# A new order for the lead and block 0 of a fused attention and two-MLP kernel, with six more groups of dummy matmuls

## The chip, the cores and the metric

The kernel runs on one core of a Trainium2 chip. The metric is device time in microseconds (us) of one execution, and of several executions the median. TensorE (PE) multiplies, VectorE (DVE), ScalarE (ACT) and GpSimd (POOL) work elementwise, and SyncE (SP) issues nearly all DMAs. Each engine runs its own instructions strictly in the order in which the program lists them, and semaphores hold an instruction until its operands are there.

## What is computed

Three layers follow one another, all in fp32:

```python
# r, k, v: (4, 8, 768, 48); w, u: (8, 48)
for t in range(S):                              # decayed linear attention
    cur = einsum('bhd,bhe->bhde', u * kt, vt)
    y[:, :, t] = einsum('bhd,bhde->bhe', rt, state + cur)
    state = w * state + einsum('bhd,bhe->bhde', kt, vt)
x = y.transpose(0, 2, 1, 3).reshape(3072, 384)
h = x @ w_in;  g = relu(h)**2;    x = g @ w_out   # 384 -> 2048 -> 384
h = x @ w_in2; g = h - tanh(h);   x = g @ w_out2  # 384 -> 2048 -> 384
```

To keep fp32 accuracy, both operands of each large product are split into a high and a low part, and three of the four cross products are formed.

## The kernel before

**Blocks.** The 3072 tokens are cut in 24 chunks of 128 and 6 blocks of 512 (four chunks each). A block of an MLP layer walks over 16 slices of the hidden dimension. For slice f, gemm1 (`h.f`, line 687) makes 9 matmuls of 512 columns, ACT and DVE apply the activation and split its result, and gemm2 (line 736 in the first layer, 860 in the second) makes another 9: six on the high part (`g2.f`), three on the low part (`g2l.f`). The attention of the next block's chunks is slipped between the slices of the first layer.

**The lead.** Chunks 0 to 3 start from an empty state and have a path of their own ahead of the first gemm1, the lead. For chunk i: `rk.i` loads r and k (line 196), `v.i` the values (214); DVE makes the product r*k (`pr.i`, 539) and scales k and r by the decay (`k.i`, 545 and 548; `r.i`, 554 and 557); PE forms the bonus sums (`pb.i`, 567), transposes k (`tp.i`, 574), makes the scores of the two head halves (`lb.2i` and `lb.2i+1`, 602), the state (`lc.i`, 650) and the output (`ly.i`, 636). Between them ACT copies out of PSUM (`lbt.i` 578, `kn.i` 584, `lst.i` 668), POOL writes a diagonal (`dg.i`, 351) and DVE masks the scores over it (`lm`, 613). ACT then writes the high part of the chunk's output into the MLP's input (`lx.i`, 659), DVE the low part (`lxl.i`, 663). `tk` (DVE, 281) and `tt` (PE, 291) build a decay table.

**Weights of the first layer.** Slice f is loaded as raw 64-bit numbers (`w.f`, line 75, five buffers) and turned into two fp32 words by ACT and DVE: `c0.f` (ACT, 89), `c1a.f` (DVE, 96), `c1b.f` (DVE, 100), `c2.f` (ACT, 115), `c3.f` (DVE, 121). `h.f` needs `c2.f` at its first matmul and `c3.f` at its seventh. In block 0 this goes on beside the matmuls; in later blocks the weights stay.

**Attention of chunks 4 to 8** lies in block 0: loads `L.i`, scaling `ar`, `ak`, `nk` (DVE 373, 391, 330), scores `b.i` (PE 432), states `sv.i` (PE 447), output `y.i` (PE 513).

**Order.** The program is written without a scheduler's freedom: `first_order`, a string of some 700 items, is walked once and each item issues its instructions, so it fixes every engine's order through the lead and block 0. After it a plain loop takes over. Items `gt` are tiny POOL copies that wait for the DVE result made last before them. Items `fl` are dummy matmuls into an unused half of a PSUM bank:

```python
def fill(n):
    for q in range(n):
        nc.tensor.matmul(side()[:, 256:512], lhsT=zero, rhs=low[0:GP].bitcast(BF16), start=True, stop=True)
"fl": lambda i: fill(4)
```

A first `fill(WARM)` stands ahead of the list, and each `fl` adds four.

Of the kernel before, what the change touches and what calls it, by code (L numbers as in the profile page):

```python
# [1161 lines left out]
```

## Time and profile before

| | |
|---|---|
| three executions | 864.67, 867.27, 870.47 us (median 867.27) |
| the profiled execution | 866.38 us, of which the trace's span is 864.6 us |
| busy share of the span | PE 99%, weight loads 81%, ACT 74%, DVE 71%, POOL 25% |
| mean granted TensorE clock of the profiled execution | 0.996 |
| first gemm1 matmul | 29.98 us after the span's start |

PE's busy share counts a pipelined matmul from its start to its end, so a busy PE may still run slower than it could; its granted clock is a column of its own. The chain that ended last is PE in 97% of the span.

### The profile page before, as it was taken

Reading aid. Unit: us, or ns where it says so; the run is one execution under the profiler, and the core shown is the slowest. Engines: PE = TensorE matmul, PEld = TensorE weight load, DVE = VectorE, ACT = ScalarE, POOL = GpSimd, SP = SyncE. Lnnn points to the kernel's source line nnn. Section 1 sums busy time; section 2 is a strip of 40 time slices with the busy share of each in tenths; the row PEclk is TensorE's granted clock in tenths of the full one; section 3 lists DMA queues with packets and bytes.
Section 4 is the critical chain, followed back from the end, with each engine's and each line's share of the span. In section 5 each row is a group of like instructions: output and inputs, shape, how many; then the busy total and the mean of one; then the engine's idle time right before and its main releaser. Section 6 shows DMA issues by size and latency. Waiting matters only on the chain.

```text
span 864.6 us, 16203 instructions
## 1 busy us (share of the span) xinstructions
PE 856.0 (99%) x6415; PEld 703.1 (81%) x6415; DVE 616.2 (71%) x1101; ACT 639.6 (74%) x1172; POOL 216.5 (25%) x235
## 2 busy tenths in 40 slices
PE   8999999999999999999999999999999999999998
PEld 6788888888888888888888788888888888888886
DVE  6999842504332340515786999999999999999997
ACT  3889575545555555556887988988988988988996
POOL 4342555545554653531010010010010010010000
PEclk8999999999999999999999999999999999999999
DMA  9874331303212220603640100200200200200100
GB/s 315 279 241 154 119 128 55 108 37 104 59 55 91 71 93 37 237 2 110 206 160 13 61 0 1 74 1 0 74 1 1 73 1 1 74 0 1 38 1 36
DMA packets 26539, 67.20 MB, mean 78 GB/s; under 512 B 3424, under 2 KB 12000, under 8 KB 26464
## 3 DMA queue, kind: packets, MB, share of 16 engines
q1 hardware_dynamic: 26176, 65.79, 22.6%
q8 instruction: 50, 0.82, 0.4%
q10 hardware_dynamic: 288, 0.39, 0.1%
q14 instruction: 25, 0.20, 0.1%
HBM read 55.94 MB, written 9.44 MB: 76 GB/s over the span
## 4 chain that ended last, share of the span: by engine, by line
PE 97%; DMA 1%; ACT 1%; DVE 1%; issue 0%; SPq 0%; DVEq 0%; ACTq 0%
PE h L687 45%; PE acc L736 23%; PE o L860 22%; PE y L513 2%; PE sp L432 1%; PE sp L447 1%; DMA first<-in_rk_dram 1%; PE sc L602 1%; PE y L636 1%; PE pt L650 0%; PE pk L567 0%; PE pk L574 0%; ACT x2s L757 0%; DVE hy L799 0%; ACT y L797 0%
## 5 line engine op out<-in xcount | busy, mean ns | idle before, releaser
L687 PE MATMUL h<-xs,w 128*128 128x512 f32 x864 | 211.3, 389 | 0.0
L687 PE MATMUL h<-xt,w 128*128 128x512 f32 x864 | 210.4, 389 | 0.1
L687 PEld LDWEIGHTS h<-xs,w 128*128 128x128 f32 x864 | 162.2, 188 | 34.0
L687 PEld LDWEIGHTS h<-xt,w 128*128 128x128 f32 x864 | 162.0, 188 | 34.0 <-ACT xt L659 0.3
L702 ACT ACTIVATE g<-h 128x512 f32<-128x512 f32 x96 | 57.3, 598 | 130.4 <-PE h L687 99.7
L736 PE MATMUL acc<-ghi,w 128*128 128x512 f32 x576 | 150.2, 394 | 0.0
L860 PE MATMUL o<-ghi,w 128*128 128x512 f32 x574 | 148.1, 390 | 0.0
L860 PEld LDWEIGHTS o<-ghi,w 128*128 128x128 f32 x574 | 107.3, 188 | 23.3 <-ACT ob L884 1.3
L736 PEld LDWEIGHTS acc<-ghi,w 128*128 128x128 f32 x576 | 106.5, 188 | 22.9 <-ACT ghi L710 0.4
L713 POOL TENSOR_TENSOR glo<-g,ghi 128x512 fp32r<-128x512 f32 x64 | 82.6, 1291 | 140.9 <-PE acc L736 78.2
L530 DVE TENSOR_TENSOR xt<-y,xt 128x384 fp32r<-128x384 f32 x20 | 11.1, 557 | 146.9 <-ACT xt L524 146.9
L778 POOL TENSOR_TENSOR xs<-x2f,xs 128x512 fp32r<-128x512 f32 x18 | 24.4, 1357 | 358.3 <-DVE xs L777 358.3
L800 ACT ACTIVATE th<-h 128x512 f32<-128x512 f32 x96 | 57.6, 600 | 41.0 <-DVE hy L799 41.0
L860 PE MATMUL o<-glo,w 128*128 128x512 f32 x287 | 83.3, 392 | 0.3 <-DVE glo L830 0.3
L736 PE MATMUL acc<-glo,w 128*128 128x512 f32 x288 | 82.2, 389 | 0.0
L813 DVE SCALAR_TENSOR_TENSOR hy<-q,hy 128x512 f32<-128x512 f32 x96 | 76.7, 799 | 0.1
L799 DVE SCALAR_TENSOR_TENSOR hy<-h,y 128x512 f32<-128x512 f32 x96 | 65.9, 687 | 14.1 <-ACT y L797 14.0
L818 DVE COPY_PREDICATED hy<-mask,th 128x512 f32<-128x512 uint8 x96 | 70.8, 738 | 0.1
L803 DVE TENSOR_TENSOR th<-h,th 128x512 f32<-128x512 f32 x96 | 66.2, 690 | 6.1 <-ACT th L800 0.7
L801 ACT ACTIVATE q<-y,ba 128x512 f32<-128x512 f32 x96 | 68.6, 714 | 0.0
L804 ACT ACTIVATE q<-y,bb 128x512 f32<-128x512 f32 x96 | 68.5, 713 | 0.0
L807 ACT ACTIVATE mask<-y,bm 128x512 uint8<-128x512 f32 x96 | 68.3, 711 | 0.0
(114 smaller groups left out, 1114.5 us busy)
## 6 DMA issues: line engine op xcount, KB each, us to landing
raw<-in_w_dram SPq DMA_DIRECT2D x32, 768.0 KB, 5.1
rkt<-in_rk_dram SPq DMA_DIRECT2D x20, 512.0 KB, 3.8
x2d<-x2s SPq DMA_DIRECT2D x18, 256.0 KB, 2.3
x2f<-x2d SPq DMA_DIRECT2D x18, 256.0 KB, 3.4
vs<-in_nat_dram SPq DMA_DIRECT2D x40, 112.0 KB, 4.1
out_dram<-ob SPq DMA_DIRECT2D x17, 256.0 KB, 2.4
rnt<-in_nat_dram SPq DMA_DIRECT2D x20, 192.0 KB, 4.2
kn<-in_nat_dram SPq DMA_DIRECT2D x20, 192.0 KB, 4.4
```

The source lines that it names most:

```text
L687: nc.tensor.matmul(h, lhsT=w_in(layer, f, part, kk), rhs=x[:, xpart, kk, :], start=(n == 0), stop=(n == 3 * KK - 1),)
L713: nc.gpsimd.tensor_tensor(lo, g, hi.bitcast(F32), op=ALU.subtract)
L736: nc.tensor.matmul(acc[j][m], lhsT=w_out(1, f, part, m * 128, (m + 1) * 128), rhs=g, start=(f == 0 and n == 0), stop=(f == NF - 1 and n == 2),
L799: nc.vector.scalar_tensor_tensor(out=hy, in0=h, scalar=PK, in1=y, op0=ALU.mult, op1=ALU.mult)
L800: nc.scalar.activation(out=th, in_=h, func=AF.Tanh)
L801: nc.scalar.activation(out=q1, in_=y, func=AF.Square, bias=p2["ba"], scale=1.0)
L803: nc.vector.tensor_tensor(th, h, th, op=ALU.subtract)
L804: nc.scalar.activation(out=q2, in_=y, func=AF.Square, bias=p2["bb"], scale=1.0)
L807: nc.scalar.activation(out=mask, in_=y, func=AF.Sign, bias=p2["bm"], scale=1.0)
L813: nc.vector.scalar_tensor_tensor(out=hy, in0=q2, scalar=PD, in1=hy, op0=ALU.add, op1=ALU.mult)
L818: nc.vector.copy_predicated(hy, mask, th)
L860: nc.tensor.matmul(acc[j][m], lhsT=w, rhs=g, start=(f == 0 and n == 0), stop=n == 2 and f == (NF - 2 if m == KK - 1 and j == NB - 1 else N ...
```

## The change

Two things differ. The number of dummy matmuls at the very start, `WARM`, goes from 28 to 27, and `first_order` is another string. The new one has the same items and six `fl` more (`fl.4` to `fl.9`): 24 more dummy matmuls in the list, 23 more in all. All else is in another order. Its first and last lines, and those of the old one:

```diff
-    WARM = 28
+    WARM = 27
...
-        pr.0 k.0 fl.2 fl.0 r.0 pb.0 tp.0 rk.1 rk.2 pr.2 k.2 v.1 v.0 fl.1 tk.0 gt.5 kn.0 tt.0 pr.1 v.2 tn.0 r.1 k.1
-        ub.0 lbt.0 lb.0 lb.1 pb.1 lbt.1 w.0 c1a.0 dg.0 lm.0 tp.1 lc.0 rk.3 lm.1 lb.2 dg.1 lm.2 kn.1 lst.0 ly.0 r.2
...
-        sq.17 hi.17 s1d.8 s1p.8 d.8 nk.9 m.8
+        tk.0 pr.0 fl.2 fl.0 pb.0 k.0 fl.4 fl.5 fl.6 tp.0 kn.0 r.0 w.0 rk.1 pr.1 r.1 ub.0 fl.1 rk.2 pr.2 lbt.0 v.1 v.0
+        v.2 tt.0 tn.0 dg.0 lb.0 c0.0 pb.1 lbt.1 lb.1 dg.1 k.1 r.2 v.3 lm.0 lm.1 gt.19 tp.1 kn.1 lb.2 lm.2 c1a.0 rk.3
...
+        nr.9 ak.9 h.17 ev.0 rl.17 ar.9 ev.2 sq.17 ns.9 d.9 gt.18 hi.17 gt.4 m.8 nk.9 gt.1
```

What that moves is seen on the engines. First PE, behind the warm-up and ahead of the first scores; before, from the bonus sums of chunk 0 on:

```order
L567 MATMUL pk<-wu,first 64x2 x8
L574 MATMUL pk<-ident,first 128x112 x4
L301 LDWEIGHTS zero
L301 MATMUL pt<-low,zero 128x256
...
L291 MATMUL pt<-ident,kh 64x48 x8
L602 MATMUL sc<-first 64x128 x16
```

and in the changed kernel, from the same place:

```order
L567 MATMUL pk<-wu,first 64x2 x8
L301 LDWEIGHTS zero
L301 MATMUL pt<-low,zero 128x256
...
L574 MATMUL pk<-ident,first 128x112 x4
...
L291 MATMUL pt<-ident,kh 64x48 x8
L602 MATMUL sc<-first 64x128 x8
L567 MATMUL pk<-wu,first 64x2 x8
L602 MATMUL sc<-first 64x128 x8
```

The dots are more dummies of the same two rows: before, four between the transposes (574) and the table (291); now twelve between the sums and the transposes, then four. Eight more stand ahead of `lc.0` and four behind `pb.3`. On DVE, `tk.0` (281) was the eighth instruction of the lead's chunk work, behind the first two chunks to arrive, and is now the first.

Second, SP's queue at the start; before:

```order
L245 DMA wu<-in_w_dram 112x16
L199 DMA first<-in_rk_dram 128x512
L196 DMA first<-in_rk_dram 128x1024 x2
L214 DMA first_v<-in_nat_dram 128x448 x3
L951 DMA ub<-in_u_dram 64x192 x2
L75 DMA raw<-in_w_dram 128x1536
L196 DMA first<-in_rk_dram 128x1024
```

and now:

```order
L245 DMA wu<-in_w_dram 112x16
L199 DMA first<-in_rk_dram 128x512
L75 DMA raw<-in_w_dram 128x1536
L196 DMA first<-in_rk_dram 128x1024
L951 DMA ub<-in_u_dram 64x192 x2
L196 DMA first<-in_rk_dram 128x1024
L214 DMA first_v<-in_nat_dram 128x448 x3
```

The raw weights of slice 0 (768 KB) go ahead of chunk 1's r and k (512 KB), and chunk 2's come behind both.

Third, DVE in block 0 between the weights of slices 2 and 3 (the rows are from `c3.2` to `c3.3`, both line 121); before:

```order
L121 TENSOR_TENSOR w_2_600<-raw,w_2_600 128x768
L96 TENSOR_SCALAR raw<-raw 128x768
L100 SCALAR_TENSOR_TENSOR raw<-raw 128x768 x2
L373 TENSOR_TENSOR rkt<-rkt,tr 112x512
L727 TENSOR_TENSOR glo<-g,ghi 128x512
L121 TENSOR_TENSOR w_3_623<-raw,w_3_623 128x768
```

and now:

```order
L121 TENSOR_TENSOR w_2_622<-raw,w_2_622 128x768
L727 TENSOR_TENSOR glo<-g,ghi 128x512
L96 TENSOR_SCALAR raw<-raw 128x768 x2
L100 SCALAR_TENSOR_TENSOR raw<-raw 128x768
L330 TENSOR_TENSOR kn_98<-kn_98,kt_tab 128x384
L100 SCALAR_TENSOR_TENSOR raw<-raw 128x768
L727 TENSOR_TENSOR glo<-g,ghi 128x512
L96 TENSOR_SCALAR raw<-raw 128x768
L121 TENSOR_TENSOR w_3_673<-raw,w_3_673 128x768
```

Two shifts, one low part and the scaling of keys (330) more stand ahead of `c3.3` there; `ar.4` (373) now stands ahead of `c3.2`.

## Rows read from the trace of the kernel before

**Rows 1.** The page: busy time of each engine, and the chain that ended last

```profile
PE 856.0 (99%) x6415; PEld 703.1 (81%) x6415; DVE 616.2 (71%) x1101; ACT 639.6 (74%) x1172; POOL 216.5 (25%) x235
...
PE 97%; DMA 1%; ACT 1%; DVE 1%; issue 0%; SPq 0%; DVEq 0%; ACTq 0%
```

**Rows 2.** Stretches: us, busy of PE, weight loads, DVE, ACT, POOL; clock; DMA share; GB/s

```profile
0.00:30.00 30.00, 25.36 (x461) 20.05 (x461) 21.61 (x49) 13.82 (x38) 16.17 (x42) 0.89 0.92 314
...
10.00:11.00 1.00, 0.28 (x10) 0.28 (x10) 1.00 (x3) 0.00 (x0) 0.31 (x1) 1.00 1.09 405
11.00:12.00 1.00, 1.00 (x41) 1.00 (x40) 0.96 (x3) 0.40 (x2) 0.09 (x1) 0.85 0.98 373
17.00:18.00 1.00, 1.00 (x24) 0.94 (x24) 0.87 (x3) 0.00 (x0) 0.00 (x0) 0.50 0.98 377
18.00:19.00 1.00, 1.00 (x32) 0.70 (x24) 1.00 (x2) 0.00 (x0) 0.00 (x0) 0.73 0.98 395
30.00:60.00 30.00, 30.00 (x190) 24.56 (x191) 29.29 (x49) 27.36 (x44) 8.70 (x13) 1.00 0.72 236
30.00:150.00 120.00, 119.98 (x1316) 98.24 (x1320) 89.08 (x184) 88.08 (x171) 54.47 (x61) 1.00 0.47 154
```

**Rows 3.** Timeline of PE, lead: start, us, engine, line, tiles, count [idle before <-releaser]

```profile
1.56 5.69 PE L301 MATMUL pt<-low,zero 112*128 112x256 bf16 x36 [1.56 <-POOL low L308]
7.18 0.63 PE L567 MATMUL pk<-wu,first 112*64 112x2 f32 x16
7.75 0.60 PE L574 MATMUL pk<-ident,first 112*128 112x112 f32 x4
8.19 0.60 PE L301 MATMUL pt<-low,zero 112*128 112x256 bf16 x4
10.72 0.49 PE L291 MATMUL pt<-ident,kh 48*64 48x48 f32 x10 [1.93 <-DVE kh L281]
...
19.20 0.67 PE L602 MATMUL sc<-first 48*64 48x128 f32 x16
19.80 0.63 PE L567 MATMUL pk<-wu,first 112*64 112x2 f32 x16
...
22.20 0.63 PE L567 MATMUL pk<-wu,first 112*64 112x2 f32 x16 [0.63 <-ACT first_kn L584]
22.69 0.54 PE L650 MATMUL pt<-first_v,first_kn 128*48 128x48 f32 x16
23.16 1.08 PE L636 MATMUL y<-am,first_v 128*32 128x128 f32 x32
24.17 0.67 PE L602 MATMUL sc<-first 48*64 48x128 f32 x16
...
29.31 0.61 PE L301 MATMUL pt<-low,zero 112*128 112x256 bf16 x4
29.98 2.35 PE L687 MATMUL h<-xt,w 128*128 128x512 f32 x9
```

**Rows 4.** Timeline of DVE, lead

```profile
8.84 0.69 DVE L539 TENSOR_TENSOR first<-first 112x512 f32<-112x512 f32 x1 [1.47 <-DMA first<-in_rk_dram]
...
13.05 1.04 DVE L96 TENSOR_SCALAR raw<-raw 128x768 uint32<-128x768 uint32 x1 [0.46 <-DMA raw<-in_w_dram]
...
26.49 1.45 DVE L613 COPY_PREDICATED am<-low,sc 128x256 f32<-128x256 uint32 x4 [0.33 <-PE sc L602]
```

**Rows 5.** Timeline of DVE, first slices of block 0

```profile
33.82 0.96 DVE L121 TENSOR_TENSOR w<-raw,w 128x768 fp32r<-128x768 f32 x1 [0.43 <-ACT w L115]
...
38.35 0.96 DVE L121 TENSOR_TENSOR w<-raw,w 128x768 fp32r<-128x768 f32 x1
...
44.30 1.03 DVE L96 TENSOR_SCALAR raw<-raw 128x768 uint32<-128x768 uint32 x2
```

**Rows 6.** Timeline of ACT, the same slices

```profile
33.67 0.64 ACT L705 ACTIVATE g<-g 128x512 f32<-128x512 f32 x1
```

**Rows 7.** Timeline of PE, the same slices

```profile
39.74 4.25 PE L687 MATMUL h<-xt,w 128*128 128x512 f32 x18
```

More of the change, by code (lines that the diff above doesn't have):

```diff
@@ L945, in decay_attention_moe_moe_kernel @@
-        sq.17 hi.17 s1d.8 s1p.8 d.8 nk.9 m.8
+        tk.0 pr.0 fl.2 fl.0 pb.0 k.0 fl.4 fl.5 fl.6 tp.0 kn.0 r.0 w.0 rk.1 pr.1 r.1 ub.0 fl.1 rk.2 pr.2 lbt.0 v.1 v.0
+        v.2 tt.0 tn.0 dg.0 lb.0 c0.0 pb.1 lbt.1 lb.1 dg.1 k.1 r.2 v.3 lm.0 lm.1 gt.19 tp.1 kn.1 lb.2 lm.2 c1a.0 rk.3
+        pr.3 fl.7 fl.8 lc.0 w.2 ly.0 lx.0 pb.2 lb.3 w.1 k.2 lb.4 lbt.2 tp.2 lst.0 lc.1 c1b.0 c2.0 lm.3 ly.1 L.4 kn.2
+        pb.3 dg.2 lm.4 r.3 lst.1 fl.9 lb.5 lbt.3 dg.3 c0.1 w.4 k.3 tp.3 c0.2 lb.6 lxl.0 lc.2 c3.0 w.3 lm.5 kn.3 lm.6
@@ new lines, in decay_attention_moe_moe_kernel @@
+        lx.1 lst.2 ly.2 lx.2 lxl.1 w.5 lb.7 lm.7 c1a.1 lc.3 lst.3 nu.4 lxl.2 ly.3 lx.3 nr.4 c1b.1 c2.1 fl.3 lxl.3
+        c1a.2 L.5 c0.4 h.0 c1b.2 rl.0 c3.1 h.1 c2.2 ar.4 sq.0 w.7 c3.2 rd.4 w.6 hi.0 lo.0 rl.1 c1a.3 c1a.4 c0.3 c1b.3
+        sq.1 hi.1 nk.4 gt.13 c1b.4 h.2 rl.2 lo.1 c1a.5 g2.0 c2.3 c3.3 ak.4 w.8 c1a.7 g2.1 g2l.0 c0.5 c2.4 c3.4 h.3
+        sq.2 c0.7 gt.17 h.4 rl.3 hi.2 c1b.5 sq.3 hi.3 gt.9 c2.5 gt.14 c0.8 lo.2 c0.6 g2.2 c1b.7 rl.4 sq.4 c2.7 gt.11
+        ns.4 d.4 c1a.8 c3.5 c1a.6 c1b.6 hi.4 b.4 sv.4 g2.3 h.5 lo.3 rl.5 c2.6 w.9 c3.7 c0.9 g2l.2 g2.4 sq.5 c1b.8 nu.5
@@ new lines, in decay_attention_moe_moe_kernel @@
+        s0p.4 c3.6 L.6 ar.6 h.7 h.6 c1a.9 gt.0 w.10 c1a.10 lo.4 ar.5 hi.5 lo.5 g2l.1 g2l.3 c2.8 g2.5 c3.8 gt.8 s0p.6
+        c1b.9 ak.5 nu.6 s1a.4 rl.6 rl.7 sq.6 s0p.5 h.8 w.12 w.11 nr.5 hi.6 m.4 g2l.4 sq.7 g2.6 lo.6 c2.9 nr.6 c3.9
+        gt.10 c1a.11 hi.7 c0.10 rl.8 c1b.10 h.9 sq.8 w.13 c2.10 s1d.4 w.14 lo.7 c3.10 c0.11 gt.15 g2.7 hi.8 g2l.5
+        g2l.6 c1a.12 lo.8 rd.5 s1p.4 c0.12 c1b.11 nk.5 rl.9 sq.9 c2.11 h.10 rl.10 ns.5 sv.5 s1a.5 c1a.14 y.4 w.15
+        sq.10 nk.6 c3.11 rd.6 b.5 c1b.12 ns.6 hi.10 hi.9 lo.10 d.5 L.7 c1a.13 g2.8 g2l.7 c2.12 h.11 s1p.5 c3.12 gt.5
@@ new lines, in decay_attention_moe_moe_kernel @@
+        ar.7 h.12 g2.10 g2.9 g2l.8 gt.6 c0.15 nu.7 d.6 lo.9 xh.4 xl.4 m.5 rl.11 sq.11 s1d.5 hi.11 sv.6 rl.12 ak.6 y.5
+        rd.7 s1a.6 c0.13 c1b.13 b.6 L.8 c1a.15 sq.12 s0p.7 c0.14 g2.11 hi.12 g2.12 g2l.10 lo.11 c1b.14 c2.13 c3.13
+        lo.12 c1b.15 c2.14 ak.7 s1p.6 xh.5 nr.7 c3.14 c2.15 h.13 nu.8 rl.13 h.14 nk.7 g2l.9 c3.15 g2l.11 s1d.6 m.6
+        xl.5 rl.14 sq.14 hi.14 sq.13 h.15 hi.13 gt.3 ns.7 d.7 sv.7 s1a.7 gt.12 lo.13 rl.15 sq.15 y.6 hi.15 lo.14 b.7
+        g2.13 gt.2 m.7 nr.8 s1d.7 xh.6 g2.14 nk.8 g2l.12 s1p.7 gt.16 g2l.13 g2l.14 lo.15 g2a.15 xl.6 ak.8 ar.8 s0p.8
@@ L946, in decay_attention_moe_moe_kernel @@
+        y.7 L.9 sv.8 ns.8 b.8 d.8 g2b.15 g2c.15 xh.7 xl.7 h.16 s1a.8 s1d.8 s1p.8 ev.1 gt.7 nu.9 rl.16 sq.16 L.10 hi.16
+        nr.9 ak.9 h.17 ev.0 rl.17 ar.9 ev.2 sq.17 ns.9 d.9 gt.18 hi.17 gt.4 m.8 nk.9 gt.1
     """
```

18 lines of the change are left out of this document (removed).

## The prediction

> **What bounds the kernel now.** I read the page first. PE is busy for 99% of the span and is 97% of the chain that ended last [rows 1], so only what shortens PE's own sequence can help. Then the busy time by stretches. From 30 to 150 us PE is busy for 119.98 of 120 us at a granted clock of 1.00 [rows 2], so block 0 holds nothing to win: its matmuls already run back to back. In the first 30 us PE is busy for 25.36 us and the mean clock is 0.89 [rows 2]. All that a new order can give back lies there.
>
> Then PE's timeline of the lead [rows 3]. The first gemm1 matmul starts at 29.98 us. I check what that time is made of by adding up the lead's own PE work at full speed, start to start of neighbouring rows:
> - 36 dummies in 7.18 - 1.56 = 5.62 us, 0.156 us each. 40 of the 44 stand on the path (the last four run beside ScalarE's last copy): 6.24 us.
> - four bonus sums of 0.57, four transposes of 0.44, eight score groups of 0.60, four states of 0.47 (22.69 to 23.16), four outputs of 1.01 (23.16 to 24.17), one table of 0.50: 2.28 + 1.76 + 4.80 + 1.88 + 4.04 + 0.50 = 15.26 us.
> - PE starts at 1.56, and the tail from 29.31 to 29.98 is 0.67 us.
>
> Together 23.73 us. The lead took 6.25 us more. PE waited 1.93 us for `kh` from DVE before 10.72 and 0.63 us for a ScalarE copy before 22.20 [rows 3]. Behind the 1.93 us the clock is still 1.00 at 10 to 11 us, 0.85 at 11 to 12, 0.50 at 17 to 18 and 0.73 at 18 to 19 [rows 2], the lower of its two levels (1.2 instead of 2.4 GHz) for about 6.8 us, in which PE was mostly busy: half of that, 3.4 us, is lost. The sum of the three is 5.96 us; the remaining 0.3 us are smaller waits. So the lead's bound is PE, slowed by one wait and by the low clock that follows it.
>
> **The change, term by term.**
>
> *Dummies.* One fewer at the start, 24 more in the list, all 24 on the path (only `fl.3` stands again beside the last copy): 23 x 0.156 = +3.6 us of PE work [rows 3]. The Trainium skill (TensorE: Matmul & The Clock Gate, Back-to-back issue gap) has 256 columns / 2.4 GHz + 2.5 ns for one matmul by itself, some 0.11 us; by it the term would be an estimated 2.5 us and the forecast 1.1 us lower. The row has 0.156 with each dummy's own weight load between, and decides.
>
> *The wait for `kh`.* `tk.0` is now the first of DVE's chunk work. PE reaches the table behind 51 dummies, one group of sums and one of transposes: 1.56 + 7.96 + 0.57 + 0.44 = 10.5 us. DVE had begun its chunk work, pushed back now by one short instruction, over 3 us before its product at 8.84 [rows 4]. The 1.93 us go.
>
> *The low clock.* From 1.56 to the first scores PE now has no wait that I can find, and dummies where it idled. In the trace the clock fell only behind the idle stretch. I take the 3.4 us as regained; the first rival takes it as not.
>
> *Loads.* The raw weights of slice 0 go ahead of chunk 1. Before, the first chunk product beyond chunk 0 waited for two loads of 512 KB and began at 8.84 [rows 4]; now it waits for 768 + 512 KB, 256 KB more. Between 8.84 and 13.05 [rows 4] three loads of values (224 KB each), 96 KB of `ub` and the 768 KB landed: 1.57 MB in 4.2 us, 374 GB/s. So `pr.1` starts at about 8.84 + 0.7 = 9.5 us and chunk 2's product 512 + 96 KB later, at 11.2. With 0.69 us for each of the products behind it, `k.1` ends at about 12.5, and PE reaches the transposes that need it at 10.5 + 0.50 + 0.60 + 0.57 + 0.60 = 12.8 us. This term is nothing on the path as long as the load is under 0.3 us late; if it is later, PE waits for just that.
>
> *What is late next.* The chain from the last scores over DVE's mask to the last output. `lb.7` ends, two masks take 0.73 us (four took 1.45 [rows 4]) and some 0.15 us of signalling, of which `lc.3` covers 0.47: about 0.4 us of wait. I add one more wait of 0.4 us, about two thirds of the 0.63 us that PE showed at full clock [rows 3], since DVE is loaded nearly as much as PE: 21.61 of the first 30 us [rows 2], and starting 3 us late.
>
> *The lead's sum*: 23.73 + 3.59 + 0.4 + 0.4 = 28.1 us, against 29.98: 1.9 us gained. From below: no wait at all, 27.3 us, 2.7 us gained. From above: both waits at 0.63 us and 0.3 us of late load, 28.9 us, 1.1 us gained.
>
> *Block 0.* DVE is busy for 29.29 of its first 30 us [rows 2], so its order matters. Before, `c3.3` ended at 38.35 + 0.96 = 39.31 us [rows 5], and `h.3` needs it at its seventh matmul, 39.74 + 6/18 of 4.25 = 41.16 us [rows 7]: a margin of 1.85 us. Between `c3.2` and `c3.3` there now stand two shifts, one low part and one key scaling more and one scaling less. A shift is half of 1.03 us [rows 5], a product of 512 columns 0.69 us [rows 4]; at an estimated 0.6 each, three net are 1.8 us. `c3.2` cannot start earlier, since it waited there for ScalarE [rows 5], and the low part behind it needs ScalarE's copy behind the square that ended at 34.31 [rows 6]. So the margin is used up, and I put 0.2 us for PE's first waits in block 0, between 0 and the 3.5 us of the second rival. The POOL copies `gt` are as many as before and hold back POOL alone, which is busy for 8.70 of those 30 us [rows 2]. Past block 0 every engine's order is the old one.
>
> *Total.* -1.9 + 0.2 = -1.7 us. Against the profiled execution's 866.38 us that is 864.7. That execution lies 0.9 us below the median of the three runs, which themselves spread over 5.8 us; I forecast 865.0 us.
>
> **Rivals.**
>
> *The clock falls all the same.* Then about 6.8 us of the lead run at half speed, and 3.4 us come back: 28.1 + 3.4 = 31.5 us, and the run takes 866.38 + 1.5 + 0.2 = 868.1 us, slower than before. It decides from 3.8 us of low clock on, since half of that is the gain. For it: the clock stayed low for 6.8 us though PE was mostly busy [rows 2, 3], with the same small matmuls that still fill the lead. Against it: no idle stretch like the 1.93 us remains ahead of them. The Trainium skill (TensorE: Matmul & The Clock Gate, Seeing it yourself and What's actually happening) has the default as the slow level and the moment of change as varying from run to run of one kernel; by that some runs could show this even where the profiled one doesn't.
>
> *PE waits for DVE in block 0.* DVE was 98% busy there and has now no margin at `c3.3`. If PE waits 0.5 us at each of `h.3` to `h.9`, 3.5 us go and the run takes 866.38 - 1.9 + 3.5 = 868.0 us, slower; it decides from 1.9 us of waits on. For it: the margin of 1.85 us turned into none. Against it: the work ahead of `c3.3` is done early, not added, so later slices find less of it.
>
> *The lead does not get shorter.* DVE's own chain is about as long as PE's: `r.2` ends at about 13.1 us, and up to the last mask there follow eight masks of 0.73 us, four products of 0.69 [rows 4], two low parts at an estimated 0.6 and slice 0's three conversions (0.52, and 0.96 twice [rows 5]), 12.2 us; the last output and the tail add 1.7: 27.0 us. Two chains of equal length that wait for each other in turn can lose the 1.9 us between them: 866.4 us, no change.
>
> **Chances and numbers.** The forecast with its bounds (lead 27.3 to 28.9 us, waits in block 0 under 1 us) 0.50, times of 863.7 to 866.3; the lead as long as before 0.20, 866.4; the clock 0.15, 868.1; DVE in block 0 0.15, 868.0. With the 0.9 us between the profiled run and the median added to the upper ones and some 2 us of spread taken off below, the range is 861.8 to 869.2 us. About 1% (8.7 us) is what a measurement of this kernel can tell from no change. No case that I can price reaches it: the lead at its bound gains 2.7 us, the two slow rivals together lose 4.9. I put 0.02 for faster, 0.95 for the same and 0.03 for slower.
>
> **What would show it.** The first gemm1 matmul near 28.1 us; no PE wait over 0.5 us before 12 us and none for `kh`; the granted clock at 1.00 through the lead (a value of 0.5 anywhere is the first rival); chunk 1's product on DVE at about 9.5 us; PE's waits between 35 and 60 us adding up to under 0.5 us, with DVE's line 121 as releaser if they are more. The forecast is wrong if the first gemm1 matmul comes after 29.5 us or before 27 us, or if block 0 loses over 1 us.

## The result and the profile after the change

The changed kernel takes 876.24 us (median of 4 runs, 874.17 to 881.19), the kernel before 866.14 us (4 runs, 864.67 to 870.47) beside it: a ratio of 1.0115, with a 95% interval of 1.0086 to 1.0143. It is slower, by 0.9 to 1.4%; the forecast was 865.0 us (861.8 to 869.2), no change.

The profiled execution took 874.17 us with a span of 872.5 us; that of before 866.38 us with 864.6. Runs of one kernel differ with their mean granted clock (before: 864.3 us at 1.00 to 873.7 us at 0.986, over all runs of this study); these two profiled ones have the same, 0.996, so they can be compared. The profiled execution of the changed kernel is the fastest of its four, so what follows accounts for 7.8 us; the medians lie 10.1 us apart.

The page of the changed kernel: busy time, the queue that carries PE's instructions (packets, MB, share), the chain that ended last.

```profile
PE 860.3 (99%) x6438; PEld 705.2 (81%) x6438; DVE 621.7 (71%) x1101; ACT 638.8 (73%) x1172; POOL 222.2 (25%) x235
...
q8 instruction: 50, 0.82, 0.4%
...
PE 90%; ACT 1%; DVE 1%; issue 0%; DVEq 0%; ACTq 0%
```

PE is 4.3 us busier than in [rows 1]; the span is 7.8 us longer (872.46 and 864.64 us from the first record of the trace to the last). The first gemm1 starts at 34.43 us instead of 29.98 [rows 3], 4.45 us later, and from there to the end it takes 838.03 us instead of 834.66, 3.4 us more. So the loss has two places, the lead and what follows it.

**The lead.** Stretches of the changed kernel, as in [rows 2] (busy of PE, weight loads, DVE, ACT, POOL; clock; DMA share; GB/s), and PE's timeline, as in [rows 3]:

```profile
0.00:30.00 30.00, 25.79 (x416) 20.06 (x416) 19.65 (x44) 11.60 (x31) 15.48 (x40) 0.89 0.82 286
7.00:8.00 1.00, 1.00 (x22) 0.76 (x20) 0.50 (x2) 0.00 (x0) 0.76 (x4) 1.00 0.80 161
8.00:9.00 1.00, 1.00 (x11) 0.90 (x10) 0.00 (x0) 0.00 (x0) 0.11 (x1) 1.00 0.71 229
...
15.00:16.00 1.00, 0.36 (x6) 0.32 (x8) 1.00 (x4) 0.45 (x1) 0.00 (x0) 0.77 1.01 387
16.00:22.00 6.00, 6.00 (x78) 4.33 (x74) 3.88 (x8) 0.13 (x1) 0.17 (x1) 0.50 1.03 365
22.00:23.00 1.00, 1.00 (x32) 0.98 (x34) 0.00 (x0) 0.59 (x3) 0.00 (x0) 0.82 1.02 294
```

```profile
7.85 1.48 PE L301 MATMUL pt<-low,zero 112*128 112x256 bf16 x12
9.17 0.55 PE L574 MATMUL pk<-ident,first 112*128 112x112 f32 x4
...
11.79 0.67 PE L602 MATMUL sc<-first 48*64 48x128 f32 x16
14.29 0.57 PE L574 MATMUL pk<-ident,first 112*128 112x112 f32 x4 [1.84 <-issue]
15.64 1.45 PE L602 MATMUL sc<-first 48*64 48x128 f32 x16 [0.77 <-DVE am L613]
...
31.09 1.36 PE L636 MATMUL y<-am,first_kn 128*32 128x128 f32 x27
33.42 0.42 PE L636 MATMUL y<-am,first_kn 128*32 128x128 f32 x5 [0.97 <-issue]
...
34.43 1.88 PE L687 MATMUL h<-xt,w 128*128 128x512 f32 x7
```

The wait for `kh` is gone. In its place PE waits 1.84 us ahead of the transposes of chunk 1 (14.29) and 0.77 us ahead of the next scores (15.64). Behind them the clock falls: 0.77 at 15 to 16 us, 0.50 up to 22, 0.82 at 22 to 23, the lower level for 6.83 us in all. At 33.42 PE pauses 0.97 us inside the last group of outputs, after 27 of its 32 matmuls, with "issue" as releaser: it waited for nothing that the profile shows.

DVE's timeline, as in [rows 4], and then POOL's in the same stretch:

```profile
10.38 0.69 DVE L539 TENSOR_TENSOR first<-first 112x512 f32<-112x512 f32 x1 [2.89 <-DMA first<-in_rk_dram]
11.18 0.93 DVE L554 TENSOR_TENSOR first<-first,tr 112x512 f32<-112x512 f32 x1
12.04 1.11 DVE L539 TENSOR_TENSOR first<-first 112x512 f32<-112x512 f32 x1
13.08 1.11 DVE L545 TENSOR_TENSOR first<-first,tr 112x512 f32<-112x512 f32 x1
14.12 1.11 DVE L554 TENSOR_TENSOR first<-first,tr 112x512 f32<-112x512 f32 x1
```

```profile
10.44 4.25 POOL L351 TENSOR_SCALAR_AFFINE_SELECT am<-bt 128x512 f32<-128x512 f32 x4 [2.32 <-ACT bt L578]
```

Chunk 1's product starts at 10.38 us, released by its load; in 7 to 9 us the loads moved only 161 and 229 GB/s. Chunk 2's load landed at 12.02, and its product starts at 12.04. And the products behind chunk 1's take 0.93 to 1.11 us instead of 0.69 [rows 4] just as long as POOL writes its four diagonals, 10.44 to 14.69 us. The decayed keys (line 545) end at 14.19; PE's transposes start 0.1 us later, so the 1.84 us ahead of them are a wait for these keys, though the row has "issue".

**Block 0.** PE's timeline at the tenth gemm1, then DVE's and POOL's ahead of it:

```profile
67.26 1.52 PE L687 MATMUL h<-xt,w 128*128 128x512 f32 x6
71.43 0.98 PE L687 MATMUL h<-xt,w 128*128 128x512 f32 x3 [2.65 <-DVE w L121]
```

```profile
62.80 0.95 DVE L100 SCALAR_TENSOR_TENSOR raw<-raw 128x768 uint32<-128x768 uint32 x1
63.67 3.58 DVE L391 TENSOR_TENSOR rkt<-rkt,tr 112x512 f32<-112x512 f32 x1
67.18 0.78 DVE L454 SCALAR_TENSOR_TENSOR s<-st,wst,sp 112x48 f32<-112x48 f32 x4
```

```profile
63.37 0.42 POOL L175 COPY turn<-w 1x1 f32<-1x1 f32 x1 [4.25 <-DVE w L121]
63.75 1.00 POOL L322 TENSOR_TENSOR rnt<-rnt,ub 128x384 f32<-128x384 f32 x1
64.72 1.98 POOL L327 TENSOR_TENSOR rnt<-rnt,kn 128x384 f32<-128x384 f32 x2
```

After six of nine matmuls PE waits 2.65 us for DVE's low words of slice 9. DVE is late because one instruction, line 391, takes 3.58 us. It is a product of two tensors of 512 columns; such products take 0.69 us elsewhere [rows 4]. It ends 0.5 us after POOL's three products, which a copy (line 175, a `gt`) had released at 63.37. The rest of PE's waits in block 0 is 0.26 us (line 447); 0.5 us of the 3.4 are no wait that the trace shows.

### The profile page after: what moved, and what is told of

The parts are those of the page before. It is cut to its first block, busy times and chain, and to the rows that moved or that the text cites. A ratio compares the mean times of both kernels' runs of the same rounds, so it can differ in the third digit from the quotient of the medians.

```text
span 872.5 us, 16256 instructions
## 1 busy us (share of the span) xinstructions
PE 860.3 (99%) x6438; PEld 705.2 (81%) x6438; DVE 621.7 (71%) x1101; ACT 638.8 (73%) x1172; POOL 222.2 (25%) x235
## 4 chain that ended last, share of the span: by engine, by line
PE 90%; ACT 1%; DVE 1%; issue 0%; DVEq 0%; ACTq 0%
PE h L687 42%; PE o L860 22%; PE acc L736 21%; PE y L513 2%; PE sp L432 1%; PE sp L447 1%; ACT x2s L757 0%; DVE hy L799 0%; ACT y L797 0%; DVE raw L100 0%; ACT q L801 0%; DVE th L803 0%; ACT th L800 0%; DVE hy L818 0%; ACT mask L807 0%
## 5 line engine op out<-in xcount | busy, mean ns | idle before, releaser
L530 DVE TENSOR_TENSOR xt<-y,xt 128x384 fp32r<-128x384 f32 x20 | 11.2, 558 | 146.8 <-ACT xt L524 146.8
```

## Experiments

All ratios are to the kernel before on the same chip, with 95% intervals. "Rest" is the time from the first gemm1 to the end of the profiled span (before: 834.66 us; the change: 838.03). Ratios are of all executions; times of single steps are of the one profiled execution.

**1. The lead alone.**

```diff
- first_order up to h.0: as before, 28 warming dummies
+ first_order up to h.0: as in the change, 27; behind it as before
```

> The changed kernel's order up to the first gemm1, then the old order of block 0. Theory: the 7.9 us that the change lost in its profiled execution are two separate losses, 4.45 us in the lead (first gemm1 matmul at 34.43 instead of 29.98 us) and about 3.3 us of PE waits in block 0, and the first belongs to the lead's order alone. Then the first gemm1 matmul comes at 34.4 us, PE has no wait over 0.5 us behind it, and the run takes about 4.5 us more than the kernel before (ratio 1.005). Rival: the wait in block 0 is the late lead carried on (weights and attention of block 0 are behind because of it); then PE waits 2 to 3 us between 60 and 80 us here too, and the ratio is about 1.009.

874.25 us, ratio 1.0073 (1.0048 to 1.0097). First gemm1 at 32.71, rest 834.8: no loss behind the lead. The profiled execution, at 869.23 us the fastest of ten, had no fall of the clock (mean 1.00), and the lead was still 2.7 us longer than before, though the two waits at chunk 1 were only 0.39 and 0.77 us. Of this, 0.9 us stand ahead of chunk 0's sums, which start at 8.12 us instead of 7.18 [rows 3]; PE's timeline shows where most of the rest is:

```profile
23.18 0.67 PE L602 MATMUL sc<-first 48*64 48x128 f32 x16
24.61 0.54 PE L574 MATMUL pk<-ident,first 112*128 112x112 f32 x4 [0.76 <-issue]
...
28.27 1.36 PE L636 MATMUL y<-am,first_kn 128*32 128x128 f32 x27
31.70 0.41 PE L636 MATMUL y<-am,first_kn 128*32 128x128 f32 x5 [2.07 <-issue]
...
32.71 1.66 PE L687 MATMUL h<-xt,w 128*128 128x512 f32 x6
```

Two pauses with "issue", 0.76 and 2.07 us. The operands of both groups were long there.

**2. Block 0 alone.**

```diff
- first_order behind h.0: as before
+ first_order behind h.0: as in the change, the lead as before
```

> The old order up to the first gemm1, then the changed kernel's order of block 0 (the five items that it had already issued in its lead stand right behind h.0). Theory: the first gemm1 matmul at 30.0 us as before, and the PE wait of about 2.7 us for a low weight part of slice 9 or 10 is there all the same, because DVE's scaling of keys (line 391) of chunk 5 takes 3.6 instead of 0.7 us while POOL runs three products: about 3 us more than the kernel before (ratio 1.003 to 1.004). Rival: the wait came from the late lead; then there is no wait over 0.5 us behind 30 us and the ratio is 1.000.

872.17 us, ratio 1.0059 (1.0042 to 1.0077). With the old lead PE waits 2.78 us at the same gemm1, behind the same instruction of DVE (3.59 us); rest 839.2, with a pause of 0.84 us ("issue") at 89.30 in it. The first gemm1 came at 31.15 us though the lead was the old one: the clock fell twice, for 6.83 and 3.41 us. Each half of the loss is there without the other, and the two ratios add up to about the whole.

**3. The load put back.** In the change, the weights of slice 0 behind the values, as before.

```diff
- r.0 w.0 rk.1 pr.1 ... v.2 tt.0 ... lb.0 c0.0 ... tp.1 kn.1
+ r.0 rk.1 pr.1 ... v.2 w.0 tt.0 ... lb.0 ... tp.1 kn.1 c0.0
```

> The changed kernel, but the raw weights of slice 0 are loaded behind three of the four loads of values, as before, and their first conversion on ScalarE (line 89) comes behind kn.1. Theory: the late loads are what lengthened the lead: chunk 1's product on DVE starts near 8 us instead of 10.4, chunk 2's near 9, PE has no wait over 0.5 us before its transposes of chunk 1, the clock stays at 1.00, and the first gemm1 matmul comes at 28 to 29.5 us; the run takes 5 to 6 us less than the changed kernel. Rival: the 24 dummies (3.7 us of PE work) are what lengthened it; then the first gemm1 matmul still comes after 32 us and the run gains under 2 us. Second rival: the clock falls in this lead whatever PE waits for; then 31 to 32 us.

873.17 us, ratio 1.006 (1.0032 to 1.0088). Chunk 1's product starts at 7.75 us instead of 10.38, every product takes 0.69 us since they now end before POOL starts (11.00), and PE has no wait up to 22 us. Then it stands still, in front of the same transposes as in experiment 1:

```profile
21.32 0.67 PE L602 MATMUL sc<-first 48*64 48x128 f32 x16
24.14 0.90 PE L574 MATMUL pk<-ident,first 112*128 112x112 f32 x4 [2.15 <-issue]
```

The clock fell to its lower level at 23.5 us, inside this pause, for 6.83 us, and the first gemm1 came at 32.42. So the late load is the cause of the early waits. In this trace taking it away brings 2 us of the lead, not 4.45. In the medians it brings more: 1.006 is about what block 0 alone costs (1.0059, experiment 2), so there little of the lead's loss is left. Rest 839.8: PE waited 3.29 us at the tenth gemm1 here, and the clock fell once more, at 71.31, for 3.41 us.

**4. The hold in block 0 moved.** POOL's copy `gt.8` behind the product that had taken 3.58 us.

```diff
- c3.8 gt.8 s0p.6 c1b.9 ak.5 nu.6
+ c3.8 s0p.6 c1b.9 ak.5 gt.8 nu.6
```

> The changed kernel with one of POOL's holding copies (gt.8) put behind ak.5 instead of behind c3.8, so that POOL's three products start only when DVE's scaling (line 391) of chunk 5 is done. Theory: that DVE instruction goes from 3.58 to 0.7 us, the PE wait of 2.65 us for line 121 goes, and the run takes 2.5 to 3 us less than the changed kernel; the first gemm1 matmul stays at 34.4 us. Rival: DVE has too much to do there in any case; then its instruction is short but PE still waits over 2 us for line 121 within the next slices.

872.69 us, ratio 1.0068 (1.0041 to 1.0095). Line 391 takes 0.69 us again; the next product of DVE, line 727, now takes 1.51 us, and PE waits 1.20, 0.30 and 0.75 us at three places. Rest 837.7: 0.4 us better than the change. The kernel before had `gt.8` behind `ak.5` too; the new order had moved it ahead.

**5. No added dummies.**

```diff
- fl.4 fl.5 fl.6 ... fl.7 fl.8 ... fl.9
```

> The change without its six added groups of four dummies; everything else is as in the change. Theory A (TensorE's instructions arrive in pieces of 127 matmuls with their weight loads; the 347th and the 474th matmul are the first of a piece, whatever they compute, and cannot start earlier than some 6 to 7 us after the 220th and the 347th): the 474th matmul now lies in the first gemm1, which is slow enough, so the pause of 0.97 us that came ahead of the 474th goes; a pause at the 347th is possible. With 3.75 us of dummies away but the late load of chunk 1 as it is (the wait ahead of the transposes of chunk 1 grows to about 3.7 us), the first gemm1 comes at 30 to 33 us instead of 34.43, block 0 still loses about 3.3 us, and the profiled time is 869.5 to 872.5 us against 874.2 of the change. Theory B (the dummies cost only their own work and the pauses belong to the data of those steps): the pauses stand at the same steps of the program, ahead of the transposes of chunk 3 and within the last outputs. Theory C (the dummies hold the clock up): without them the low clock lasts longer and the first gemm1 is no earlier than 34 us.

876.23 us, ratio 1.0093 (1.0059 to 1.0127). No pause ahead of the 474th matmul (it is now in a gemm1), as theory A had it. But PE waits 0.56 and 2.00 us ahead of 14.3 us and the clock stays at its lower level from 13.21 us on for 20.5 us; first gemm1 at 36.31. Theory C had that, but experiment 8 shows the same 20.5 us with the dummies in place, so it is not shown that they hold the clock up. The ratio is not told apart from that of the change: the dummies did not cost the 1%.

Block 0 did not lose the 3.3 us that were expected: rest 835.8, 1.1 us more than before, though its order is that of the change. POOL's copy (65.26 us) took 1.03 us instead of 0.42 and ended with line 391, so POOL's products started behind line 391, which took 0.69 us, and the wait of 2.65 us is not there. Lines 454 and 465 then ran beside these products at their usual 0.79 and 1.84 us.

```profile
65.56 0.69 DVE L391 TENSOR_TENSOR rkt<-rkt,tr 112x512 f32<-112x512 f32 x1
```

```profile
66.25 1.00 POOL L322 TENSOR_TENSOR rnt<-rnt,ub 128x384 f32<-128x384 f32 x1
```

So one order can fall either way here, and where line 391 and the products do not meet, 2.3 of the 3.4 us are gone.

**6. `kh` first, nothing else.**

```diff
- pr.0 k.0 fl.2 ... fl.1 tk.0 gt.5
+ tk.0 pr.0 k.0 fl.2 ... fl.1 gt.5
```

> The kernel before with one step moved: the product of the table kh is the first of VectorE's chunk work. Both theories: the wait of 1.93 us for kh goes. Theory A (pieces of 127 matmuls): TensorE is 2 us early at its 220th matmul and pauses ahead of its 347th with all data ready, by 1 to 2.4 us in place of the 0.2 us of the kernel before, in the middle of a group of scores; so of 1.93 us of wait and up to 3.4 us of low clock only a part comes back: the first gemm1 at 27 to 28.5 us, and 1.5 to 3 us less than the kernel before at the same granted clock (863.5 to 865 us in a run like its profiled one of 866.4). Theory B (no such pause): the first gemm1 at 25 to 26 us, 862 us. Theory D (the wait moves to the next product that TensorE needs): a VectorE wait of over 1 us appears before 15 us and the first gemm1 comes at 29.5 us or later, no gain.

866.9 us, ratio 1.0013 (0.999 to 1.0036). Theory D came: the wait for `kh` turned into 2.85 us ahead of chunk 1's transposes, and the first gemm1 came at 30.92. TensorE and ScalarE are earlier, so POOL's diagonals start earlier (11.32 us instead of 11.91) and meet a product of DVE:

```profile
11.36 2.89 DVE L554 TENSOR_TENSOR first<-first,tr 112x512 f32<-112x512 f32 x1
```

```profile
11.32 2.38 POOL L351 TENSOR_SCALAR_AFFINE_SELECT am<-bt 128x512 f32<-128x512 f32 x4
```

**7. Earlier load, no added dummies, old block 0.** Experiment 3's lead without `fl.4` to `fl.9` and with 28 warming dummies, then block 0 as before.

```diff
- first_order of the change
+ experiment 3 up to h.0 without fl.4 to fl.9; behind it as before
```

> A lead out of the change's order with two edits (the weights of slice 0 loaded behind the values as before, their first shift behind the second chunk's copy; and none of the six added groups of dummies), and behind the first gemm1 the block 0 of the kernel before. Theory A: no wait ahead of chunk 1's transposes, a pause of 1 to 2.4 us ahead of the 347th matmul with its data ready, none ahead of the 474th, no waits over 0.5 us in block 0; the first gemm1 at 26 to 28 us, and 2 to 4 us less than the kernel before at the same granted clock (862.5 to 864.5 us in a run like its profiled one). Theory B (the pauses belong to the data of their steps): pauses ahead of chunk 3's transposes and inside the last outputs of about the size seen with the dummies, and the first gemm1 at 28.5 to 29.5 us. Theory C (the dummies hold the clock up): the clock falls and the first gemm1 comes at 30 us or later.

865.44 us, ratio 0.9985 (0.9966 to 1.0005): the best of the study, but not told apart from the kernel before. First gemm1 at 29.35. The products run beside POOL again (1.11 us each), PE waits 0.89 and 0.77 us, the clock is at its lower level for 6.83 us. None of the three theories had this wait.

**8. Experiment 4, and the merge of chunk 4 behind slice 9.**

```diff
- m.4 ... c2.9 nr.6 c3.9
+ c2.9 nr.6 c3.9 m.4
```

> The change with GpSimd's hold of block 0 behind the decayed keys of chunk 5 (as in the earlier run with that edit) and in addition VectorE's merge of chunk 4 (1.84 us) put behind the weights of slice 9, the step that TensorE's tenth gemm1 waits for. Theory E (in block 0 the new order has no margin on VectorE at slice 9, and whatever stands ahead of it there is paid by TensorE): the wait of 1.2 us ahead of that gemm1 goes to under 0.2 us and the waits of 0.3 and 0.75 us behind it stay within 0.3 us of that; block 0 loses about 1.3 to 1.8 us instead of 2.7. Theory F (GpSimd's products running beside VectorE are the whole loss, and they will only meet another instruction): an instruction of VectorE of over 1.4 us still stands ahead of the weights of slice 9, the wait stays over 0.8 us, and block 0 loses 2.5 us or more.

876.33 us, ratio 1.0105 (1.0071 to 1.014), rest 837.4. POOL's products now meet lines 727 and 121 (1.48 and 1.77 us). The wait at the tenth gemm1 is down to 0.12 us, as theory E had it, but PE waits 0.56 us at the next gemm1 and 1.42 us at line 447, and block 0 loses 2.7 us, as theory F had it. The lead is the change's, and its first gemm1 came at 38.84: the clock was at its lower level for 20.48 us.

**9. A hold in the lead, on top of experiment 7.**

```diff
- rk.1 pr.1 r.1 ub.0 ... rk.2 pr.2 ... dg.0 ... k.1 r.2 v.3 lm.0 lm.1
+ rk.1 pr.1 k.1 r.1 gt.5 ub.0 ... rk.2 ... dg.0 ... v.3 lm.0 lm.1 pr.2 r.2
```

> The earlier kernel with the weights of slice 0 behind the values, without the added dummies and with the block 0 of before, plus three moves in the lead: a hold of GpSimd behind the second chunk's decayed r and k, those two ahead of the third chunk's product, and the products of the third chunk behind the first chunk's masks. Theory G (VectorE's products with two inputs, 0.69 us alone, take 1.11 us or once 2.89 us while GpSimd writes its diagonals, and the waits and the low clock of the lead follow from that): every such product before 12 us takes 0.7 us, TensorE has no wait over 0.5 us ahead of the transposes and scores of chunk 1, the clock stays at full from 15 to 22 us, a pause of 1 to 2.5 us comes ahead of TensorE's 347th matmul with its data ready, and the first gemm1 at 26 to 27.5 us instead of 29.35; 860.5 to 862.5 us in a run at a granted clock of 1.00, where the kernel before has 864.8. Rival H (the diagonals come too late behind the hold): TensorE waits over 1 us for the masks ahead of the second scores, the clock falls, the first gemm1 at 29 us or later and no gain over the kernel before.

866.23 us, ratio 1.0002 (0.9989 to 1.0015). The products of chunk 1 take 0.69 us, PE has no wait over 0.5 us before 15 us and the clock is 1.00 up to 24 us, as theory G had it. A pause of 0.22 us came ahead of the 220th matmul (15.47), a wait of 0.98 us at 16.88, 0.1 us behind a product of DVE (line 545) that took 1.12 us beside POOL's diagonals, and then the pause, at another step than in experiments 1, 3 and 4, after three of 16 matmuls of a group:

```profile
21.21 0.67 PE L602 MATMUL sc<-first 48*64 48x128 f32 x16
21.81 0.29 PE L650 MATMUL pt<-first_v,first_kn 128*48 128x48 f32 x3
24.51 0.51 PE L650 MATMUL pt<-first_v,first_kn 128*48 128x48 f32 x13 [2.41 <-issue]
```

It lasted 2.41 us, the clock fell behind it for 3.41 us, and the first gemm1 came at 30.28. Theory G's time failed.

**10. A hold in the lead of the change** (`gt.5`, taken from block 0).

```diff
- dg.0 lb.0 ... dg.1 k.1 r.2 v.3 lm.0 lm.1
+ lb.0 ... k.1 gt.5 dg.0 dg.1 v.3 lm.0 lm.1 r.2
```

> The change with one thing put back in its lead: a hold of GpSimd behind the decayed keys of chunk 1, ahead of the four diagonals of chunks 0 and 1, with chunk 1's decayed r behind the first masks as in the kernel before; the late load and the dummies stay. Theory G: the products of chunk 2 and the decayed keys take 0.7 us instead of 1.11, the keys end at about 13.3 us instead of 14.2, the waits of 1.84 and 0.77 us become about 1.0 and under 0.6, and the first gemm1 comes at 32 to 33.6 us instead of 34.43 (the lower end if the clock stays at full, with pauses ahead of the 347th and the 474th matmul); block 0 loses its 3.3 us as before, 871.5 to 873.5 us in a run at the clock of the profiled one of the change. Rival I (the late load of chunk 1 is the whole delay): the keys end no earlier than 14 us and the first gemm1 comes at 34 us or later.

875.44 us, ratio 1.0097 (1.0071 to 1.0124). The products take 0.69 us and the keys end at 13.58 us, as theory G had it; but waits of 1.25 and 0.68 us remain, a pause of 1.33 us stands ahead of the 474th matmul, the clock is low for 10.24 us, and the first gemm1 comes at 35.7. The late load alone leaves waits of this size; that it alone brings the low clock is not shown, since experiments 1 and 4 have the same load and no fall.

**11. POOL's products in block 0 behind slice 9.**

```diff
- c3.8 gt.8 ... ak.5 nu.6 ... nr.5 ... c2.9 nr.6 c3.9
+ c3.8 ... ak.5 ... c2.9 c3.9 gt.8 nu.6 nr.5 nr.6
```

> The change with GpSimd's hold of block 0 and the three products that it releases (u and r of chunks 5 and 6) put behind the weights of slice 9. Theory J (the three products beside VectorE's two-input instructions are the loss): the 3.58 us instruction takes 0.7 us, no instruction of VectorE takes over 1 us between 61 and 69 us, the wait of 2.65 us ahead of the tenth gemm1 goes to under 0.3 us, and block 0 loses under 1.2 us instead of 3.3; the lead is that of the change (first gemm1 near 34.4 us) and the profiled time some 2 to 3 us below 874.2. Rival K (the order has no margin anyway, and the products meet the next two-input instruction wherever they go): the waits move to the ScalarE and VectorE steps behind slice 9 and block 0 loses 2.5 us or more.

874.39 us, ratio 1.01 (1.0074 to 1.0126), rest 837.7. The wait at the tenth gemm1 is 0.23 us, as theory J had it, but the sum is theory K's: the three products meet line 727 instead, and PE waits 0.62 us at the next gemm1 and 1.45 us at line 447.

```profile
71.61 2.77 DVE L727 TENSOR_TENSOR glo<-g,ghi 128x512 fp32r<-128x512 f32 x1
```

```profile
70.86 1.01 POOL L322 TENSOR_TENSOR rnt<-rnt,ub 128x384 f32<-128x384 f32 x1
71.83 1.98 POOL L327 TENSOR_TENSOR rnt<-rnt,kn 128x384 f32<-128x384 f32 x2
```

**12. Four of POOL's products left out** (u and r of chunks 5 and 6 are not applied).

```diff
- nu.5 ... nu.6 ... nr.5 ... nr.6
```

> The change without four of GpSimd's products of block 0 (u and r of chunks 5 and 6 are left out altogether, so the keys of these chunks are used as loaded); the order of all else stays. Theory J (the products beside VectorE's two-input instructions are the loss): the 3.58 us instruction takes 0.7 us, TensorE's waits in block 0 add up to under 0.8 us, and from the first gemm1 to the end the run takes under 835.5 us, where the change has 838.1 and the kernel before 834.6. Theory K (VectorE's order and the later weights have no margin, whatever GpSimd does): waits of 2 us or more remain, 837 us or more. In between, both. The lead is that of the change (first gemm1 at 34 to 35 us).

872.56 us, ratio 1.007 (1.0042 to 1.0097), rest 836.2, between the theories. Line 391 takes 0.69 us, and the wait at the tenth gemm1 is down to 0.5 us:

```profile
59.44 0.56 DVE L96 TENSOR_SCALAR raw<-raw 128x768 uint32<-128x768 uint32 x1 [2.35 <-DMA raw<-in_w_dram]
...
63.46 0.69 DVE L391 TENSOR_TENSOR rkt<-rkt,tr 112x512 f32<-112x512 f32 x1
```

```profile
PE h L687 <- DVE w L121: 0.5, 1, 0.5
```

Of the 3.4 us that the change loses behind the lead, 838.0 - 836.2 = 1.8 us go with these products. 1.6 us stay; DVE also idles 2.35 us for late raw weights there (0.57 us in the change), which before it did not, but that this is the rest was not tried.

**13. Experiment 9 with chunk 4's loads later.**

```diff
- w.1 ... L.4 ... w.5 lb.7
+ w.1 ... w.5 L.4 lb.7
```

> The kernel with the hold in the lead (earlier loads, no added dummies, block 0 of before) with one more move: the loads of chunk 4 (1.1 MB) behind the raw weights of slice 5, and the product of GpSimd that uses them behind them. Theory L (TensorE's next instructions queue behind the loads on the DMA engines): with fewer bytes ahead, the 347th matmul comes 1 us or more sooner after the 220th than the 9.0 us seen there (8.0 us or less), its pause shrinks from 2.4 us to under 1.4 us, the clock stays at full, and the first gemm1 comes at 27.5 to 29.3 us instead of 30.28. Rival M (a piece of instructions takes 7 to 9 us in this stretch however many loads are queued): 8.5 to 9.5 us, a pause of 2 us or more, first gemm1 at 30 to 30.6 us. In both, GpSimd's later product could delay chunk 4 in block 0; then waits of TensorE for chunk 4 appear between 40 and 60 us.

866.82 us, ratio 0.9991 (0.9975 to 1.0008). Waits of 0.78 and 1.05 us came ahead of 17.2 us and the clock fell at 18.54 for 10.24 us, so PE was too slow to run dry and the pause could not show at the 347th: it came 9.3 us after the 220th without one. The wait of 0.78 us is such a pause itself, ahead of the 220th (see below). The packet for the 347th landed at 21.49, 5.8 us after the 220th matmul, in experiment 9 at 23.03, 7.6 us after it. That points to theory L, but it is one trace of each.

**14. `kh` first and the hold behind the keys.**

```diff
- tk.0 gt.5 kn.0 tt.0 ... r.1 k.1 ub.0
+ kn.0 tt.0 ... r.1 k.1 gt.5 ub.0     (tk.0 stands first)
```

> The kernel before with the table kh first on VectorE, as in the earlier run, and the hold of GpSimd in the lead moved behind the decayed keys of chunk 1. Theory G (the product of 2.89 us beside GpSimd's diagonals cost that run its gain): every product takes 0.7 us, the wait of 2.85 us ahead of chunk 1's transposes shrinks to under 0.9 us, and the first gemm1 comes at 27 to 28.8 us instead of 30.9 (before: 29.98), with a pause ahead of the 347th matmul if the clock stays at full; 1 to 2.5 us less than the kernel before at the same granted clock, a ratio of 0.997 to 0.999. Rival N (the pace at which TensorE's instructions come, or the clock, takes what is won): the waits shrink as said, but the first gemm1 comes at 29.3 us or later, and the ratio is 0.999 to 1.001.

867.16 us, ratio 0.9994 (0.9977 to 1.0012). The numbers are rival N's. The products take 0.69 us and the early waits are 0.28 and 0.27 us. PE's timeline and two stretches of it:

```profile
8.48 0.63 PE L567 MATMUL pk<-wu,first 112*64 112x2 f32 x16
...
12.41 0.60 PE L574 MATMUL pk<-ident,first 112*128 112x112 f32 x4 [0.28 <-ACT bt L578]
...
13.88 1.37 PE L602 MATMUL sc<-first 48*64 48x128 f32 x16 [0.27 <-DVE am L613]
...
20.83 0.77 PE L567 MATMUL pk<-wu,first 112*64 112x2 f32 x16 [0.63 <-ACT first_kn L584]
...
29.98 1.20 PE L687 MATMUL h<-xt,w 128*128 128x512 f32 x4
```

```profile
14.00:17.00 3.00, 3.00 (x48) 2.09 (x48) 2.82 (x8) 0.60 (x4) 1.14 (x2) 0.56 1.00 414
...
21.00:24.00 3.00, 3.00 (x64) 2.55 (x62) 1.66 (x4) 1.60 (x3) 1.58 (x2) 0.53 1.02 353
```

The clock fell all the same, at 14.35 and at 21.18 us for 3.41 us each, ahead of the second fall with only a wait of 0.63 us. The first gemm1 starts at 29.98 us, to the hundredth where it was before, but that is chance. The record of the granted clock begins at 7.52 us here and at 4.88 in the kernel before, and up to it each warming dummy takes 0.21 us, behind it 0.11. So chunk 0's sums start at 8.48 instead of 7.18 [rows 3], and from there to the first gemm1 it is 21.50 us instead of 22.80: 1.30 us gained, more than in any other run. The interval of the ratio is too wide to show so little.

**What the pauses are.** PE's instruction queue carried 50 packets in 0.82 MB, 16 KB each (page above). From the single records of the trace, with matmuls counted from 0 (us; "landed" is the end of the last such packet ahead of the matmul):

```
kernel    93rd   220th   landed  pause  the 220th is
exp. 9    9.94   15.47   14.10   0.22   13th of 16 scores
exp. 13   9.79   15.68   14.41   0.78   13th of 16 scores
         220th   347th                  the 347th is
before   19.58   25.90   24.61   0.17   4th matmul of a group of scores
exp. 1   18.70   24.61   23.12   0.76   transposes of chunk 3
exp. 3   16.84   24.14   22.86   2.15   transposes of chunk 3
exp. 4   18.96   24.98   23.70   0.87   transposes of chunk 3
exp. 9   15.47   24.51   23.03   2.41   4th matmul of a group of states
exp. 11  21.64   27.39   26.00   0.60   transposes of chunk 3
exp. 12  21.25   26.72   25.41   0.33   transposes of chunk 3
         347th   474th                  the 474th is
change   27.42   33.42   32.01   0.97   28th of 32 outputs
exp. 1   24.61   31.70   30.03   2.07   28th of 32 outputs
exp. 4   24.98   31.81   30.28   1.79   28th of 32 outputs
exp. 10  28.28   34.70   33.02   1.33   28th of 32 outputs
exp. 11  27.39   33.94   32.36   1.52   28th of 32 outputs
exp. 12  26.72   32.45   30.97   0.70   28th of 32 outputs
```

The pause stands at a count, not at a step: at the 220th, 347th and 474th matmul, 127 apart, and 1.3 to 1.7 us after a packet has landed. The two in block 0, in experiment 2 (0.84 us) and 5 (0.29 us), stand at the 983rd and 982nd record, which is 4 x 127 behind the 474th within one record, and as long after a packet. Each such matmul in the lead came 5.5 to 9.0 us after the one 127 earlier. Where PE gets there later than about 1.5 us after the landing there is no pause. In the kernel before the first gemm1 starts with the 460th matmul; the added dummies moved the 474th into the lead and so brought a second pause.

**How far one trace carries.** The change and experiments 1, 4, 8, 11 and 12 have the same lead, item by item. Their first gemm1 comes at 34.43, 32.71, 32.81, 38.84, 34.95 and 33.45 us, with the clock at its lower level for 6.83, 0, 0, 20.48, 6.83 and 3.41 us behind the start. The start differs too: the record of the clock begins between 4.67 us (experiment 7) and 7.54 us (experiment 4), and chunk 0's sums start between 7.08 and 8.48 us (7.18 before, 7.28 in the change). So a difference of 2 us between the leads of two traces is not an effect of the order by itself. The waits whose releaser a trace names, and the ratios of all executions, stand on more than that.

## Why the prediction was wrong

The prediction had 1.7 us less; 7.8 us more came. Its own lower bound of the lead, 27.3 us without any wait, with what the trace shows put on it gives 27.3 + 1.84 + 0.77 + 0.97 + 6.83/2 = 34.3 us, against 34.43. So the waits are what the sum lacked; that it closes to 0.1 us is partly luck, as the next point shows.

- **Wait for `kh`**: right, it went.
- **Dummies, 0.156 us each**: too dear. The 36 dummies behind that figure ran at two speeds, 0.21 us each up to 4.88 us, where the record of the granted clock begins, and 0.11 behind. The twelve added in a row in the change took 9.17 - 7.85 = 1.32 us, 0.11 each, the figure that the prediction had set aside. All 24 took 2.84 us in experiment 1, where the clock did not fall, and 3.68 in the change, where eight of them ran at the lower level (1.82 us), which the 6.83/2 above counts a second time.
- **Loads, "nothing on the path"**: the first step that failed. I let 256 KB more cost 0.7 us at 374 GB/s. Chunk 1's load landed at 10.36 us, its product started at 10.38 instead of 9.5, and chunk 2's at 12.04 instead of 11.2, since the loads did not hold that rate (161 and 229 GB/s in 7 to 9 us). That is about half of the 1.7 us by which chunk 1's keys came late (14.19 instead of 12.5). Experiment 3 shows it: with the old load order the product starts at 7.75, the waits before 22 us are gone and the ratio falls from 1.0115 to 1.006.
- **Durations on DVE**: failed. I took 0.69 us for every product, though the trace of before has one of 0.88 us (line 554 at 21.11) beside two diagonals of POOL that took 3.02 us instead of 1.22. Two of the lead's three `gt` copies were moved out of it, and I counted such copies at nothing because they hold back POOL alone. What they did was to keep POOL from running beside DVE's products: beside it these took 1.11 us (change), 2.89 us (experiment 6) or 3.58 us (block 0), and up to chunk 1's keys 0.69 us where a hold stood (experiments 9, 10, 14).
- **The low clock, "regained"**: failed. It came with new waits, and in experiment 14 it came without any wait like the old one, while in experiments 1 and 4 it did not come behind waits of 0.39 and 0.77 us. The first rival (0.15) named this; what decides whether it falls is not explained by the idle time alone, and stays open.
- **The late chain, 0.4 us, and the second wait, 0.4 us**: the first did not come; the second came as the 0.77 us for a mask at 15.64. What the prediction did not have at all is that PE's instructions ran out. I had no row for it but one: in the kernel before, 0.17 us of "issue" in the middle of a group of scores, for which no operand was missing:

```profile
25.30 0.43 PE L602 MATMUL sc<-first 48*64 48x128 f32 x3
25.90 1.09 PE L602 MATMUL sc<-first 48*64 48x128 f32 x29 [0.17 <-issue]
```

- **Block 0, 0.2 us**: the second rival's size (3.5 us) was right, its place was not: one wait at the tenth gemm1, not seven of 0.5 us from the fourth on. Over half of it is POOL's products (1.8 us in experiment 12, 2.3 in experiment 5), which I had set aside with the sentence on the `gt` copies. What the other 1.1 to 1.6 us are stays open.
- **The chances**: the two slow rivals together made 4.9 us in my text, and I gave their joint case almost nothing. Both came, with the load on top. A part of both has one cause that I did not see: the new order had moved the holds.
- **The gain itself was small.** Experiments 7, 9, 13 and 14 take away one wait after the other, and all lie within 0.9985 and 1.0002: in their traces most of what the lead wins at the front is taken by the pace at which PE's instructions come and by the clock.

## What to carry to other kernels

An instruction that only makes an engine wait is part of the schedule: before a step is moved past it, ask which two engines it kept apart, and price the products on the other engine at what they take when both run. In a stretch of very many small matmuls, count them; the supply of instructions can be the bound, and earlier data then bring nothing. A duration read as a mean over a warm-up holds two speeds. And two rivals of one sign that share a cause deserve a joint chance.
